# First-pair argmax by heads, bf16 one-hot in SBUF, four-pass similarities and a new order table

## The chip, the cores and the metric

The kernel runs on one core of a Trainium2 chip. The metric is device time in microseconds from the start to the end of one execution; for the kernel before it is 694.47 us, the median of three runs (694.42 to 694.76). In the text TensorE is PE, VectorE is DVE, ScalarE is ACT, GpSimd is POOL, and SP is the engine whose queue issues most DMAs.

## What is computed

Clustered attention over 2 batches x 8 heads, 768 tokens, 64 channels a head, and then two feed-forward blocks over the 1536 tokens. Only the attention is touched by the change:

```python
c_n = centroids / (norm(centroids) + 1e-06)            # 16 clusters for each head
q_assign = argmax(einsum('bhsd,hcd->bhsc', q_n, c_n))  # k_assign in the same way
mask = q_assign[:, :, :, None] == k_assign[:, :, None, :]
scores = where(mask, scale * q @ k.T, -1e9)
attn = softmax(scores); out = attn @ v
x = max(max(x @ w1, x @ w2), x @ w3) @ w_out           # first block
h = maximum(x @ w_in, 0); out = (h * h) @ w_out2       # second block
```

## The kernel before

**Numbers.** A value is held as two parts, hi (rounded to the fast matmul's format) and lo (the rest), so that a product takes three passes: hi by hi, hi by lo, lo by hi.

**Pairs.** Heads go in 8 pairs. For each pair q and k arrive (`load_qk`), are split into hi and lo (`p_rq`, `p_rk`, `p_lq`, `p_lk`), and are laid out per head by DMA into "stacks" (`p_stack`, tiles `ste` for the even head and `stodd` for the odd one). `p_sim` multiplies them with the centroids `cb`: six matmuls of 64x384 for each half of 384 tokens, accumulated in one PSUM bank (three for q, three for k). `p_simc` scales the result on ACT into SBUF (`simt`), `p_argt` transposes it on PE into PSUM, and five DVE instructions find the argmax: the maximum of each group of 16 (`p_arg0`), equal to it (`p_arg1`), times a descending weight (`p_arg2`), maximum again (`p_arg3`), equal to that (`p_arg4`). All of them work on the PSUM tile, and only the last writes a bf16 one-hot tile `oh`. `p_mkt` transposes the one-hot rows, and `p_mq`, `p_mk`, `p_m4`, `p_md` place them as 16 further rows of the stacks, where they add a large negative number to every pair of tokens in different clusters: the mask costs no pass of its own.

**The first pair** goes in two halves of 384 tokens (`hv`): its transposes, its five argmax steps and its mask rows run once for each half, and the halves alternate on DVE. The first score tile needs all of both.

**Score tiles.** Each head has 6 tiles of 128 queries, 96 in all. A tile `S` (`a_scores`) is four matmuls into a two-bank PSUM tile; there are two such tiles (ring "S", `psd`). DVE takes the row maximum (`a_max`, L738), ACT the exponential with its sum (`a_exp`, L745). Three tiles form a group: ACT and DVE make the reciprocals (`a_guard`, `a_rec`), POOL (at the start ACT) scales (`a_norm`), and for six blocks of 128 keys PE transposes (`a_tr`, L768), ACT and DVE split the block into hi and lo (`a_hi` L774, `a_lo` L779), and PE multiplies with v (`a_av`, L788 and L789). Transposes, similarities, argmax and mask transposes share three PSUM banks (ring "T", `pss`); a fourth bank collects the products with v.

**Warm-ups.** `warm(n)` (L325) issues n matmuls on the identity whose result is not used. `WARM` says how many stand at each place of the start.

**Order.** All steps of the attention are entries of a table `ops`; `ATT_ORDER` lists their numbers in the order in which they are issued. Each engine has one queue and works in that order. The feed-forward blocks follow, in an order that `arrange` works out; its first products (L425) already stand between the last attention steps.

Of the kernel before, what the change touches and what calls it, by code (L numbers as in the profile page):

```python
# [1439 lines left out]
```

## Time and profile before

| | before |
|---|---|
| median of three runs | 694.47 us |
| profiled execution, its own time | 693.93 us |
| its span, first to last instruction | 692.1 us |
| PE busy in the span | 676.9 us, 98% |
| DVE busy | 561.2 us, 81% |
| ACT busy | 501.1 us, 72% |
| POOL busy | 210.0 us, 30% |

The shares are averages over very different stages. The first 15 us bring in q and k of the first pair and find its clusters. From there to about 254 us the score tiles run; from 254 us on the feed-forward blocks do. A matmul's record reaches from its start to its result, so that records of neighbours overlap, and a busy PE is not a PE at its peak: the distance from start to start says what an instruction costs its queue. The same holds to a smaller degree for DVE and ACT.

### The profile page before, as it was taken

What the parts mean: (1) busy time and instruction counts of PE and PEld (TensorE: products, weight loads), DVE (VectorE), ACT (ScalarE), POOL (GpSimd) and SP (SyncE); (2) the same over time, 40 slices, a digit from 0 to 9 for tenths busy, and PEclk for the clock granted to TensorE, in tenths of its full rate; (3) what the DMA queues carried; (4) which work ended last, traced back from release to release, by engine and by line L of the source; (5) the groups of instructions that cost most, each with busy time, mean ns of one, the idle gap of its engine ahead of it and who ended that gap; (6) DMA issues with size and microseconds to landing.
All of it is one profiled execution on the core that took longest, in us unless ns stands there. A gap on an engine that the chain in (4) does not pass through costs nothing.

```text
span 692.1 us, 10148 instructions
## 1 busy us (share of the span) xinstructions
PE 676.9 (98%) x3531; PEld 577.3 (83%) x3531; DVE 561.2 (81%) x906; ACT 501.1 (72%) x977; POOL 210.0 (30%) x242
## 2 busy tenths in 40 slices
PE   7899999999999999999999999999999999999997
PEld 6689889899999878888888888888888888888885
DVE  6898999999999979998979659889679585968433
ACT  6899989899999865575545547798877786776610
POOL 6477987988769770100000000000000010000010
PEclk9999999999999999999999999999999999999999
DMA  7884553726432002211311231112211203120012
GB/s 207 198 234 119 120 161 91 189 58 147 111 89 91 1 1 93 91 62 61 103 66 61 76 121 62 61 62 82 101 62 61 98 27 115 48 79 1 1 73 111
DMA packets 22004, 62.21 MB, mean 90 GB/s; under 512 B 3616, under 2 KB 5280, under 8 KB 21504
## 3 DMA queue, kind: packets, MB, share of 16 engines
q1 hardware_dynamic: 21232, 59.98, 29.3%
q10 hardware_dynamic: 720, 1.57, 0.7%
q8 instruction: 28, 0.46, 0.3%
q14 instruction: 24, 0.20, 0.1%
HBM read 38.83 MB, written 3.15 MB: 61 GB/s over the span
## 4 chain that ended last, share of the span: by engine, by line
PE 62%; DVE 2%; issue 1%; ACT 1%; POOL 0%; ACTq 0%; POOLq 0%
PE pss L1066 23%; PE psn L1066 18%; PE pss L1321 10%; PE psn L1321 8%; PE pss L1142 1%; DVE acc_acc L1349 1%; DVE at L779 0%; DVE wtv L399 0%; PE pss L768 0%; ACT e L745 0%; PE pss L788 0%; PE pss L789 0%; POOL xT L822 0%; PE psn L1142 0%; PE psn L425 0%
## 5 line engine op out<-in xcount | busy, mean ns | idle before, releaser
L779 DVE TENSOR_TENSOR at<-pss,at 128x384 fp32r<-128x384 f32 x192 | 100.0, 548 | 13.1 <-ACT at L774 12.4
L763 POOL TENSOR_SCALAR e<-e,nm 128x768 f32<-128x768 f32 x93 | 85.6, 934 | 47.2 <-DVE nm L753 32.6
L738 DVE TENSOR_REDUCE nm<-psd 128x1 f32<-128x768 f32 x96 | 90.6, 948 | 5.4 <-PE psd L731 3.7
L774 ACT CAST at<-pss 128x384 fp32r<-128x384 f32 x192 | 86.5, 483 | 9.3 <-PE pss L768 7.4
L745 ACT ACTIVATE e<-psd,nm 128x768 f32<-128x768 f32 x96 | 87.3, 910 | 4.1 <-DVE nm L738 3.5
L768 PE MATMUL pss<-ident,e 128*128 128x128 f32 x576 | 86.5, 275 | 3.4 <-DVE at L779 1.7
L768 PEld LDWEIGHTS pss<-ident,e 128*128 128x128 f32 x576 | 68.6, 140 | 15.2 <-DVE at L779 5.0
L788 PE MATMUL pss<-at,vs 128*128 128x384 f32 x192 | 71.2, 371 | 0.5 <-ACT avt L801 0.5
L1321 PE MATMUL pss<-w_wh,g_g 128*128 128x512 f32 x216 | 71.4, 389 | 0.0
L789 PE MATMUL pss<-at,vs 128*128 128x384 f32 x192 | 65.8, 343 | 0.4 <-DVE at L779 0.3
L1057 POOL TENSOR_TENSOR t_tt<-a_a,t_tt 128x256 f32<-128x256 f32 x3 | 2.5, 848 | 191.5 <-DVE t_tt L1054 191.5
L1321 PE MATMUL psn<-w_wh,g_g 128*128 128x512 f32 (+1 forms) x172 | 56.5, 384 | 0.0
L1321 PEld LDWEIGHTS pss<-w_wh,g_g 128*128 128x128 f32 x216 | 40.5, 188 | 8.4
L1066 PE MATMUL pss<-xT,w_wh 128*128 128x512 f32 x140 | 43.1, 389 | 0.0
L1321 PE MATMUL pss<-w_wl,g_g 128*128 128x512 f32 x108 | 42.0, 389 | 0.0
L1042 ACT CAST w_wh<-a_a 128x1024 fp32r<-128x1024 f32 (+1 forms) x28 | 28.6, 1020 | 14.9 <-DVE a_a L1036 14.9
L789 PEld LDWEIGHTS pss<-at,vs 128*128 128x128 f32 x192 | 36.4, 189 | 3.0 <-DVE at L779 2.5
L1025 ACT ACTIVATE a_a<-raw_raw 128x512 f32<-128x512 f32 (+1 forms) x56 | 36.4, 653 | 3.3 <-DMA raw_raw<-w 1.3
L1321 PEld LDWEIGHTS psn<-w_wh,g_g 128*128 128x128 f32 x172 | 32.1, 188 | 6.4
L788 PEld LDWEIGHTS pss<-at,vs 128*128 128x128 f32 x192 | 36.2, 189 | 1.4 <-issue 0.5
L1027 ACT ACTIVATE r_r<-raw_raw 128x512 uint32<-128x512 uint32 (+1 forms) x56 | 36.5, 651 | 0.7 <-PE pss L1066 0.7
L1030 DVE SCALAR_TENSOR_TENSOR a_a<-raw_raw,a_a 128x512 uint32<-128x512 uint32 (+1 forms) x56 | 35.6, 668 | 0.5
(249 smaller groups left out, 1743.0 us busy)
## 6 DMA issues: line engine op xcount, KB each, us to landing
raw_raw<-w SPq DMA_DIRECT2D x16, 512.0 KB, 4.0
raw_raw<-win SPq DMA_DIRECT2D x16, 512.0 KB, 4.0
raw_raw<-wo SPq DMA_DIRECT2D x16, 512.0 KB, 3.6
raw_raw<-wo SPq DMA_DIRECT2D x8, 384.0 KB, 3.3
out<-acc_acc SPq DMA_DIRECT2D x11, 256.0 KB, 2.0
tv<-vv SPq DMA_DIRECT2D x7, 384.0 KB, 3.3
stodd<-rl SPq DMA_DIRECT2D x12, 192.0 KB, 5.5
stodd<-rl SPq DMA_DIRECT2D x4, 576.0 KB, 7.9
```

The costliest lines, as they stand in the source:

```text
L738: dve.tensor_reduce(nms[g][:, 0, i : i + 1], pss[s][:, :, :HS], axis=AX.XY, op=ALU.max, negate=True)
L745: act.activation(two(e), pss.pop(s)[:, :, :HS], AF.Exp, bias=nm[:, 0, i : i + 1], accum_out=nm[:, 1, i : i + 1])
L763: (pool if w == "P" else dve).tensor_scalar(e, e, r, 1.0, op0=ALU.mult, op1=ALU.mult)
L768: pe.transpose(pt[:, i * P : (i + 1) * P], et[3 * g + i][:, kt * P : (kt + 1) * P], ident)
L774: act.copy(a[:, 0, :], pts[g, kt][:, :HS])
L779: eng.tensor_tensor(a[:, 1, :], pts.pop((g, kt))[:, :HS], f(a[:, 0, :]), op=ALU.subtract)
L788: pe.matmul(avs[g][:, :HS], l, a[:, 0, :], start=kt == 0, stop=False)
L789: pe.matmul(avs[g][:, :HS], l, a[:, 1, :], start=False, stop=kt == NQ - 1)
L1025: op(("ab", u), due - 9, {A_: act_t(n) + 0.03}, lambda e, raw=raw, c=c: e.activation(T[a][:, c], f(T[raw][:, :n, 1]), AF.Abs), [("ld", u)] ...
L1027: op(("rd", u), due - 7.5, {A_: act_t(n) + 0.03}, lambda e, raw=raw, c=c: e.mul(u32(T[r][:, c]), T[raw][:, :n, 0], float(2.0**-29)), [("ld ...
L1066: pe.matmul(T[bank], T[w[wi]][:, wb * P : wb * P + P], x(xi), start=first and n == 0, stop=last and n == 3 * len(ks) - 1, skip_group_check ...
L1321: pe.matmul(T[bank][:, : n.stop - n.start], T["g", 2 * g + j, c][:, a_, i * P : i * P + P], T[wt, u][:, 512 * j + n.start : 512 * j + n.stop],
```

## The change

The first pair's argmax is taken by heads instead of by halves: the even head's five steps run over all 768 tokens (every second group of 16), then the odd head's. Its one-hot rows are transposed in four pieces, each into a PSUM tile of its own (k first half, k second half, q, and all for the odd head); q's piece goes to a two-bank score tile. The two mask rows of q and the two of k are divided anew between DVE and ACT. Score tile 1 goes to two banks of ring "T" instead of a two-bank tile (`SPLIT`), with two maxima, two exponentials and two small joining steps. For all pairs the equality, the weighting and the second maximum of the argmax now stand in the bf16 tile `oh` in SBUF. From pair 1 on (`WIDE`) a similarity half takes four matmuls instead of six: the hi and lo centroids stand side by side in `cb`, so that one pass over a hi input makes 128 rows (hi in one half of them, lo in the other), and a new DVE step `p_simd` adds the two halves of rows after ACT has scaled one of them. The first pair's first k remainder moves from DVE to POOL, two small steps of the centroid norm stand earlier, its scale is copied to four groups of 32 rows instead of two, and the warm-ups go from 98 to 70. Several `after` entries are dropped or changed, and the order table is new.

```diff
-WARM = 12, 34, 0, 28, 10, 14, 0
+WARM = 12, 24, 0, 34, 0, 0, 0
+SPLIT = 1,
-    "lk@0": "D", ...
+    "lk@0": "PD", ...
+WIDE = 1
 ATT_ORDER = [
-    4, 7, 5, 6, 11, 12, 8, 9, 50, 13, 20, 14, 0, 16, 22, 3, 21, 15, 23, 24, 25, 18, 33, 26, 2, 17, 34, 1, 27, 51, 19, 35,
+    4, 7, 6, 12, 5, 8, 11, 9, 13, 52, 20, 14, 0, 16, 22, 1, 21, 15, 23, 24, 18, 25, 2, 17, 26, 3, 27, 19, 53, 28, 29, 54,
...
-    cb = ac.tile([P, 2, HP, 96], F32R, name="cb")
+    cb = ac.tile([P, HP, 160], F32R, name="cb")
...
             ops = []
-            for w, hs, ls in ((slice(32, 96), 0, 3), (slice(0, 64), 1, 2)):
-                ops += [(cb[:, 0, hp, w], rl[:, hs, c]), (cb[:, 0, hp, w], rl[:, ls, c]), (cb[:, 1, hp, w], rl[:, hs, c])]
-            for i, (l, r) in enumerate(ops):
-                pe.matmul(pt[0:64, :HS], l, r, start=i == 0, stop=i == 5)
+            for w, hs, ls in ((32, 0, 3), (0, 1, 2)):
+                ops += [(w, 64, ls), (w, 128, hs)] if p >= WIDE else [(w, 64, hs), (w, 64, ls), (w + 64, 64, hs)]
+            ops.sort(key=lambda o: -o[1])
+            for i, (w, n, x) in enumerate(ops):
+                pe.matmul(pt[0:n, :HS], cb[:, hp, w : w + n], rl[:, x, c], start=i == 0, stop=i == len(ops) - 1, skip_group_check=True)
...
+        def p_simd(p, hf):
+            r = slice(64 * hf, 64 * hf + 64)
+            t = simt[p][r]
+            dve.scalar_tensor_tensor(t, psims[p, hf][r, :HS], scl[r, p % HP : p % HP + 1], t, op0=ALU.mult, op1=ALU.add)
...
-            dve.tensor_tensor(arg_in(p, c), arg_in(p, c), argm[p][:, c].unsqueeze(2).to_broadcast([P, n, NC]), op=ALU.is_equal)
+            dve.tensor_tensor(one_hot(p, o), arg_in(p, o), by_group(argm[p], o), op=ALU.is_equal)
...
-            dve.tensor_tensor(arg_in(p, c), arg_in(p, c), tieb.unsqueeze(1).to_broadcast([P, c.stop - c.start, NC]), op=ALU.mult)
+            t = one_hot(p, o)
+            dve.tensor_tensor(t, t, tieb.unsqueeze(1).to_broadcast([P, t.shape[1], NC]), op=ALU.mult)
...
+            if i == 2:
+                pt = pmk["q"] = rings["S"][1][:, 0, :].bitcast(BF16)
+            else:
+                pt = pmk["k", i] = ps_m(f"pmk{p}_{i}", BF16)
...
-            act.activation(st[0][64:80, 1, half(hf)], pmk[p][0:16, half(hf)], AF.Identity, bias=m4b[0:16], scale=m4s[0:16])
+            to, fr = st[0][64:80, 1, QS[i]], pmk["q"][0:16, QS[i]]
+            if i == 0:
+                dve.tensor_scalar(to, fr, BIG, -BIG, op0=ALU.mult, op1=ALU.add)
+            else:
+                act.activation(to, fr, AF.Identity, bias=m4b[0:16], scale=m4s[0:16])
...
-            dve.tensor_copy(st[0][64:80, 3, half(hf)], pmk["k"][0:16, half(hf)])
+            (act.copy if hf else dve.tensor_copy)(st[0][64:80, 3, half(hf)], pmk["k", hf][0:16, half(hf)])
...
+            if s in SPLIT:
+                pt = [ps_t(f"ps{s}_{hf}")[:, :HS] for hf in range(2)]
...
+            for hf, to in enumerate((m, part[:, 0:1])):
+                dve.tensor_reduce(to, pss[s][hf], axis=AX.X, op=ALU.max, negate=True)
+            dve.tensor_tensor(m, m, part[:, 0:1], op=ALU.min)
```

On DVE the first pair's argmax reads as follows before, from its first maximum (`mx`, `m` and `oh` are its maxima and its one-hot tile, `pss_69` the transposed similarities, `ste` the even head's stack, `nm` the score tiles' maxima):

```order
L653 TENSOR_REDUCE mx_247<-pss_69 128x12
L658 TENSOR_TENSOR pss_69<-pss_69,mx_247 128x192
L653 TENSOR_REDUCE mx_247<-pss_69 128x12
L662 TENSOR_TENSOR pss_69<-pss_69,tieb 128x192
L658 TENSOR_TENSOR pss_69<-pss_69,mx_247 128x192
L667 TENSOR_REDUCE m_295<-pss_69 128x12
L662 TENSOR_TENSOR pss_69<-pss_69,tieb 128x192
L673 TENSOR_TENSOR oh_299<-pss_69,m_295 128x192
L667 TENSOR_REDUCE m_295<-pss_69 128x12
L673 TENSOR_TENSOR oh_299<-pss_69,m_295 128x192
L697 CAST ste_228<-pss_71 16x384 x2
```

And now, on DVE from the same maximum to the first score tiles' maxima:

```order
L681 TENSOR_REDUCE mx_288<-pss_69 128x12
L684 TENSOR_TENSOR oh_294<-pss_69,mx_288 128x12x16
L688 TENSOR_TENSOR oh_294<-oh_294,tieb 128x12x16
L692 TENSOR_REDUCE m_299<-oh_294 128x12
L696 TENSOR_TENSOR oh_294<-oh_294,m_299 128x12x16
L681 TENSOR_REDUCE mx_288<-pss_69 128x12
L731 CAST ste_221<-pss_70 16x384
L726 TENSOR_SCALAR ste_221<-psd_80 16x128
L684 TENSOR_TENSOR oh_294<-pss_69,mx_288 128x12x16
L688 TENSOR_TENSOR oh_294<-oh_294,tieb 128x12x16
L692 TENSOR_REDUCE m_299<-oh_294 128x12
L779 TENSOR_REDUCE nm_340<-psd_76 128x1
```

The even head's one-hot rows are ready after five instructions instead of ten, and the odd head's five stand behind the first mask copies.

On ACT the same place before, from the copies that fill the even stack (`m` is the mask for the odd head, `e` the exponentials):

```order
L573 CAST ste_228<-rl_201 64x1536
L481 DMA tv_318<-vv 128x768
L694 ACTIVATE ste_228<-pss_70,m4b,m4s 16x384 x2
L702 ACTIVATE m_353<-pss_70,m4b,m4s 64x768
L745 ACTIVATE e_371,nm_360<-psd_76,nm_360 128x768
L745 ACTIVATE e_373,nm_360<-psd_80,nm_360 128x768
L619 ACTIVATE simt_379<-pss_69,scl 64x384
L745 ACTIVATE e_394,nm_360<-psd_76,nm_360 128x768
L749 ACTIVATE nm_360<-nm_360,guard 128x3
```

And now on ACT:

```order
L585 CAST ste_221<-rl_194 64x1536
L488 DMA tv_307<-vv 128x768
L728 ACTIVATE ste_221<-psd_80,m4b,m4s 16x640
L731 CAST ste_221<-pss_71 16x384
L792 ACTIVATE e_344,nm_340<-psd_76,nm_340 128x768
L736 ACTIVATE m_359<-pss_71,m4b,m4s 64x768
L795 ACTIVATE e_367,nm_340<-pss_69,nm_340 128x384
L795 ACTIVATE e_367,part<-pss_70,nm_340 128x384
L792 ACTIVATE e_374,nm_340<-psd_80,nm_340 128x768
L804 ACTIVATE nm_340<-nm_340,guard 128x3
```

One mask copy of k stands behind the long one of q, the odd head's mask stands behind the first exponential, and the second exponential is in two pieces.

## Rows read from the trace of the kernel before

**Rows 1.** Busy us of each engine by stretch (start:end, length; x instructions).

```profile
150.00:200.00 50.00, 49.92 (x334) 46.98 (x335) 46.99 (x85) 47.92 (x115) 39.68 (x43) 1.00 0.49 115
200.00:250.00 50.00, 48.50 (x304) 42.67 (x302) 46.53 (x80) 44.39 (x105) 39.03 (x40) 1.00 0.14 47
300.00:350.00 50.00, 50.00 (x222) 41.40 (x221) 47.14 (x68) 28.74 (x46) 0.74 (x1) 1.00 0.24 85
```

**Rows 2.** Timeline, two bursts on PE: start, length, engine, line, tiles, count.

```profile
124.86 1.08 PEld L768 LDWEIGHTS pss<-ident,e 128*128 128x128 f32 x9
...
127.07 1.22 PE L613 MATMUL pss<-xT,cb 128*64 128x384 f32 x6
```

**Rows 3.** PE's weight loads by line, 50 to 250: busy, mean | idle before.

```profile
L768 PEld LDWEIGHTS pss<-ident,e 128*128 128x128 f32 x516 | 61.8, 140 | 11.2 <-DVE at L779 4.1 <-POOL xr L810 0.9 <-POOL e L763 0.9
L789 PEld LDWEIGHTS pss<-at,vs 128*128 128x128 f32 x171 | 32.4, 189 | 2.8 <-DVE at L779 2.3
L788 PEld LDWEIGHTS pss<-at,vs 128*128 128x128 f32 x171 | 32.3, 189 | 1.4 <-issue 0.5 <-ACT avt L801 0.4
```

**Rows 4.** DVE by line, 50 to 250 us.

```profile
L779 DVE TENSOR_TENSOR at<-pss,at 128x384 fp32r<-128x384 f32 x172 | 89.5, 548 | 10.6 <-ACT at L774 10.0
L738 DVE TENSOR_REDUCE nm<-psd 128x1 f32<-128x768 f32 x81 | 76.6, 948 | 2.9 <-PE psd L731 2.2
```

**Rows 5.** DVE by line and shape, 0 to 260 us: the argmax and a remainder.

```profile
L658 DVE TENSOR_TENSOR pss<-pss,mx 128x384 f32<-128x384 f32 x7 | 3.9, 564 | 0.2
L662 DVE TENSOR_TENSOR pss<-pss,tieb 128x384 f32<-128x384 f32 x7 | 3.9, 559 | 0.0
L667 DVE TENSOR_REDUCE m<-pss 128x24 bf16<-128x384 f32 x7 | 3.9, 555 | 0.1
...
L559 DVE TENSOR_TENSOR rl<-tk,rl 128x384 fp32r<-128x384 f32 x2 | 1.1, 545 | 0.0
...
L662 DVE TENSOR_TENSOR pss<-pss,tieb 128x192 f32<-128x192 f32 x2 | 0.7, 366 | 0.1
```

**Rows 6.** Timeline from the first warm-ups to the second score tile.

```profile
1.68 1.46 PE L325 MATMUL pss<-identb 128*128 128x128 bf16 x12 [1.68 <-DVE identb L318]
...
3.73 3.23 PE L325 MATMUL pss<-identb 128*128 128x128 bf16 x34
...
6.77 2.29 PE L613 MATMUL pss<-rl,cb 128*64 128x384 f32 x12
...
8.19 0.58 ACT L619 ACTIVATE simt<-pss,scl 64x384 f32<-64x384 f32 x1 [1.13 <-DVE scl L503]
...
9.42 0.36 DVE L653 TENSOR_REDUCE mx<-pss 128x12 f32<-128x192 f32 x1 [1.33 <-PE pss L644]
...
9.93 0.37 PE L644 MATMUL pss<-ident,simt 64*128 64x64 f32 x3 [0.54 <-DVE mx L653]
...
10.23 1.74 PE L325 MATMUL pss<-identb 128*128 128x128 bf16 x28
...
13.13 0.34 PE L688 MATMUL pss<-identb,oh 128*32 128x128 bf16 x3 [1.16 <-DVE oh L673]
13.37 0.36 DVE L673 TENSOR_TENSOR oh<-pss,m 128x192 bf16<-128x192 f32 x1
...
15.02 1.22 ACT L694 ACTIVATE ste<-pss,m4b,m4s 16x384 fp32r<-16x384 bf16 x2 [2.61 <-PE pss L690]
...
16.82 0.52 PE L731 MATMUL psd<-ste 80*128 80x384 f32 x2
```

**Rows 7.** Timeline of ACT, the first exponentials and their scaling.

```profile
16.25 0.99 ACT L702 ACTIVATE m<-pss,m4b,m4s 64x768 fp32r<-64x768 bf16 x1
17.76 0.90 ACT L745 ACTIVATE e<-psd,nm 128x768 f32<-128x768 f32 x1 [0.52 <-DVE nm L738]
...
22.97 1.75 ACT L761 ACTIVATE e<-e,nm 128x768 f32<-128x768 f32 x2
...
28.41 0.92 ACT L745 ACTIVATE e<-psd,nm 128x768 f32<-128x768 f32 x1
```

More of the change, by code (lines that the diff above doesn't have):

```diff
@@ L290, in single_banks @@
     def single_banks(i):
-        pd[i].close()
-        one = ctx.enter_context(tc.tile_pool(name=f"pn{i}", bufs=1, space=PSUM, side=SIDES[i]))
+        o = (i + len(SPLIT)) % 2
+        pd[o].close()
+        one = ctx.enter_context(tc.tile_pool(name=f"pn{i}", bufs=1, space=PSUM, side=SIDES[o]))
         psu[i][:2] = [one.tile([P, 512], F32, name=f"psn{2 * i + j}") for j in range(2)]
@@ L498, in clustered_attention_moe @@
         cs = ap1.tile([P, 4], F32, name="cs")
-        scl = ap1.tile([64, HP], F32, name="scl")
+        scl = ap1.tile([P, HP], F32, name="scl")
         def c_scale(eng, i):
-            for r in (0, 32):
+            for r in range(0, P, 32):
                 eng.tensor_copy(scl[r : r + 32, i : i + 1], cs[32 * i : 32 * i + 32, 3:4])
@@ L516, in clustered_attention_moe @@
         ]
-        parts = [lambda o=o, r=r, c=c: act.copy(cb[r, 0, :, c], pcv[r, :, o, :]) for o, r, c in rc]
-        parts += [lambda o=o, r=r, c=c: dve.tensor_tensor(cb[r, 1, :, c], pcv[r, :, o, :], f(cb[r, 0, :, c]), op=ALU.subtract)
+        parts = [lambda o=o, r=r, c=c: act.copy(cb[r, :, c], pcv[r, :, o, :]) for o, r, c in rc]
+        parts += [lambda o=o, r=r, c=c: dve.tensor_tensor(cb[r, :, c.start + 64 : c.stop + 64], pcv[r, :, o, :], f(cb[r, :, c]), op=ALU.subtract)
                   for o, r, c in rc]
@@ L541, in p_rk @@
         def p_rk(p, hf=0):
+            prepared(p)
             c = halves(p)[hf]
@@ L669, in p_arg4, with of_head @@
-        def p_arg4(p, hf=None):
-            c = tiles_of(hf)[1]
-            o = once(oh, p, lambda: ap1.tile([P, NB_, NC], BF16, tag="oh", name=f"oh{p}"))
-            n = c.stop - c.start
-            dve.tensor_tensor(o[:, c], arg_in(p, c), argn[p][:, c].unsqueeze(2).to_broadcast([P, n, NC]), op=ALU.is_equal)
+        def of_head(t, o):
+            if o is None:
+                return t
+            return t.rearrange("p (u h) -> p u h" if len(t.shape) == 2 else "p (u h) c -> p u h c", h=2)[:, :, o]
@@ L675, in clustered_attention_moe, with p_mkt @@
         pmk, mrow = {}, {}
-        def p_mkt(p, hf=None):
-            pt = once(pmk, p, lambda: ps_m(f"pmk{p}", BF16))
+        def p_mkt(p, i=None):
             if p:
+                pt = pmk[p] = ps_m(f"pmk{p}", BF16)
                 o = oh[p].rearrange("p (t a) c -> p t (a c)", t=NQ // 2)
-                for i in range(NQ // 2):
-                    pe.transpose(pt[:, i * P : (i + 1) * P], o[:, i, :], identb)
+                for t in range(NQ // 2):
+                    pe.transpose(pt[:, t * P : (t + 1) * P], o[:, t, :], identb)
@@ new lines, in p_mkt, with p_mq @@
+            for t in range(NQ):
+                if i > 1 or t // (NQ // 2) == i:
+                    c = slice(0, 64) if i == 3 else slice(0, 16) if i == 2 else slice(32, 48)
+                    pe.transpose(pt[0 : c.stop - c.start, t * P : (t + 1) * P], o[:, t, c], identb)
+            if i == 3:
+                pmk[p] = pt
+            warm(WARM[4])
+        QS = [slice(0, P), slice(P, S)]
+        def p_mq(p, i):
+            to, fr = st[0][64:80, 1, QS[i]], pmk["q"][0:16, QS[i]]
[3 more added lines that the diff above has]
+                act.activation(to, fr, AF.Identity, bias=m4b[0:16], scale=m4s[0:16])
@@ L720, in clustered_attention_moe @@
         et, nms, pss, ats, avs, xraw, pts = {}, {}, {}, {}, {}, {}, {}
+        part = ap1.tile([P, 2], F32, name="part")
         def a_scores(s):
@@ L724, in a_scores @@
             t = st[h]
-            pt = ps_s(f"ps{s}")
+            if s in SPLIT:
+                pt = [ps_t(f"ps{s}_{hf}")[:, :HS] for hf in range(2)]
+            else:
+                pt = ps_s(f"ps{s}")
+                pt = [pt[:, hf, :HS] for hf in range(2)] + [pt[:, :, :HS]]
             k2 = slice(0, 80) if h % 2 == 0 else slice(0, 128)
@@ L744, in a_exp, with a_sum @@
             nm = nms[g]
-            act.activation(two(e), pss.pop(s)[:, :, :HS], AF.Exp, bias=nm[:, 0, i : i + 1], accum_out=nm[:, 1, i : i + 1])
+            pt, m, sm = pss.pop(s), nm[:, 0, i : i + 1], nm[:, 1, i : i + 1]
+            if s not in SPLIT:
+                act.activation(two(e), pt[2], AF.Exp, bias=m, accum_out=sm)
+                return
+            for hf, to in enumerate((sm, part[:, 1:2])):
+                act.activation(e[:, half(hf)], pt[hf], AF.Exp, bias=m, accum_out=to)
+        def a_sum(s):
+            g, i = divmod(s, 3)
+            sm = nms[g][:, 1, i : i + 1]
+            dve.tensor_tensor(sm, sm, part[:, 1:2], op=ALU.add)
         def a_guard(g):
@@ L870, in clustered_attention_moe @@
                      opens=[("sm", p, 0)] if hf == 0 else (), uses=[("T", "sim", p, hf), ("sm", p, 0)])
+                if p >= WIDE:
+                    pop_("simd", p_simd, (p, hf), [("simc", p, hf)], uses=[("T", "sim", p, hf), ("sm", p, 0)])
+            sims = [("simd" if p >= WIDE else "simc", p, h) for h in range(2)]
             for hf in hv:
-                first = hf != (1,)
-                sim = [("simc", p, h) for h in (hf or (0, 1))]
-                pop_("argt", p_argt, (p, *hf), sim, opens=[("T", "arg", p)] * first, uses=[("sm", p, 0), ("T", "arg", p)])
@@ new lines, in clustered_attention_moe @@
+            for o in [(0,), (1,)] if p == 0 else [()]:
+                first = o != (1,)
+                pop_("arg0", p_arg0, (p, *o), [("argt", p, *hf) for hf in hv], uses=[("T", "arg", p)])
+                pop_("arg1", p_arg1, (p, *o), [("arg0", p, *o)], opens=[("oh", p)] * first, uses=[("oh", p), ("T", "arg", p)])
+                pop_("arg2", p_arg2, (p, *o), [("arg1", p, *o)], uses=[("oh", p)])
+                pop_("arg3", p_arg3, (p, *o), [("arg2", p, *o)], uses=[("oh", p)])
+                pop_("arg4", p_arg4, (p, *o), [("arg3", p, *o)], uses=[("oh", p)])
@@ new lines, in clustered_attention_moe @@
+            if p == 0:
+                for i in range(4):
+                    pop_("mkt", p_mkt, (p, i), [("arg4", p, i // 3)] + [("mkt", p, i - 1)] * (i > 0), opens=[("T", "mk" if i == 3 else f"mk{i}", p)] * (i != 2), uses=[("oh", p)])
+                for hf in range(2):
+                    pop_("mk", p_mk, (p, hf), [("mkt", p, hf), ("stack", p, 0)], uses=[("T", f"mk{hf}", p)])
+                for i in range(2):
+                    pop_("mq", p_mq, (p, i), [("mkt", p, 2), ("stack", p, 0)])
+            else:
+                pop_("mkt", p_mkt, (p,), [("arg4", p)], opens=[("T", "mk", p)], uses=[("oh", p)])
```

117 lines of the change are left out of this document (55 added, 62 removed), and 143 rows, old and new, of tables (ATT_ORDER, ENG).

## The prediction

> **What bounds the kernel now.** I read the busy times by stretch first. From 300 us on, PE's records cover 50.00 of 50 us [rows 1]: a microsecond that the attention gives back before 254 us reaches the end, since the work behind it is PE's own and the change leaves its order alone. The question is what sets the pace before 254 us. There PE is again nearest to full, 49.92 of 50 us from 150 to 200, but ACT has 47.92 and DVE 46.99 in the same stretch [rows 1], so no engine has much room. PE's records overlap; two matmuls of 384 columns take 0.52 us and six take 1.22 [rows 2, 6], so one costs (1.22 - 0.52) / 4 = 0.175 us of the queue, and a transpose 1.08 / 9 = 0.12 us [rows 2]. From 50 to 250 us the weight loads of the transposes and of the two value products wait 11.2 + 2.8 + 1.4 = 15.4 us [rows 3]; part of that lies beside running matmuls. PE is thus full to something between 92 and 98%, and its largest named wait is for DVE's remainder (L779), which holds a bank of ring "T". DVE in turn stands idle 10.6 + 2.9 = 13.5 us there, 10.0 of it behind ACT's cast of the same bank [rows 4]. This is a loop of PE, ACT and DVE over three banks in which PE is tightest and DVE second. The start is another matter: there one chain decides, from the similarities through the argmax to the first score tile.
>
> **The first pair.** Before, the sims start at 6.77 us because 34 warm-ups stand ahead of them, the scale is ready for the first copy at 8.19, the second half's transposes end at 9.93 + 0.37 = 10.30, the last one-hot row at 13.37 + 0.36 = 13.73, and score tile 1 ends at 16.82 + 0.52 = 17.34 [rows 6]. Now ten warm-ups fewer free about 10 x 3.23 / 34 = 0.95 us of the queue, of which I take 0.55, as the remainders must be there too (POOL now makes one of them). The transposes then end at about 9.75. Five steps of 192 elements at 0.36 to 0.37 us [rows 5, 6] and a few hundredths between them make 2.0 us, so the even head's one-hot is there at 11.75, although it waits for both halves. Three transposes of one-hot rows took 0.34 us, the last one's way out in it [rows 6]; twelve at some 0.09 and that way out end at 13.0. Then ACT, in the order shown, makes 640 columns of q's mask (0.87 us, between 1.22 / 2 = 0.61 for 384 [rows 6] and 0.99 for 768 [rows 7]) and after it one half of k's (0.5): 14.4. The score tiles end at 14.6 and 15.2, 2.1 us earlier than before. The 34 warm-ups after the transposes (about 34 x 1.74 / 28 = 2.1 us [rows 6]) end at about 11.8, just as the one-hot is ready; where they run longer, they delay it by as much.
>
> Not all of the 2.1 us stays. Followed on, ACT makes the odd head's mask (0.99) between the first two exponentials, since DVE puts the last step of that argmax behind the first maximum; tile 1's exponential comes in two pieces; the group's guard waits for the sum's joining step, which is queued on DVE behind two maxima and a remainder. I get the group's scaling on ACT ending near 23.2 instead of 22.97 + 1.75 = 24.72, then both similarity copies of pair 1 (0.58 each, as at 8.19 [rows 6]) where one stood, and the seventh exponential at 27.75 by ACT's queue and 28.1 by DVE's, against 28.41 [rows 7]. DVE has by then done about 1 us more of pair 1's argmax. Between the 0.3 us at that mark and the 2.1 at tile 1, and with this 1 us, I take **-1.3 us**; bounds 0 and -2.5 (the 2.1 and the rest of the 0.95). The odd head's mask DMAs stand behind two loads of pair 2 on SP now; those rows are needed only at score tile 6, at about 25 us by this count, so I cost them at nothing; without that cover it is the time of the two loads.
>
> **Four-pass similarities.** Seven pairs, two halves, two matmuls fewer: 28 x 0.175 = 4.9 us off PE. It would all reach the end if PE were full alone. With PE at 92 to 98% and the other two engines close behind, I let 60% through: **-2.9 us**; bounds 0 and -4.9.
>
> **DVE.** `p_simd` adds 14 instructions on 64x384. The trace has none of its kind; the nearest are the remainders of the same length, 0.548 us [rows 4] and 0.545 from SBUF [rows 5]. Records of neighbours overlap by some 0.09 us, so 14 cost 6.4 to 7.7 us of DVE. Against it stands the argmax in bf16. From 384 to 192 elements the weighting falls from 559 to 366 ns [rows 5], about 1 ns an element; the remainder costs as much from SBUF (545) as the weighting from PSUM (559), so by rows the place alone buys nothing, and the gain is from 0 to what half the elements would save, 0.19 us for a step. I take that for the weighting alone: 7 x 0.19 = 1.3 us. DVE's net load is some 5 us more. It lies in the 13.5 us in which DVE stands idle [rows 4], so I cost it at **0**; bounds -1 and +5.2 (6.5 - 1.3), the latter if the idle time is tied to ACT's casts and can't be filled.
>
> The Trainium skill (VectorE: DVE Perf Modes, The perf-mode tier table) says that a two-tensor operation runs at twice the rate where all its tensors are 16-bit in SBUF, and that a reduction never does. By it the weighting is faster and the second maximum is not, which is what I took; the two equalities have an operand that is repeated or in fp32, and are left as they are. No run here shows a bf16 step in SBUF yet.
>
> **Banks.** A similarity bank is now held through ACT's copy and DVE's addition, about 0.6 us longer, 14 times: 8 us of bank time. The argmax bank is free after the second of five steps instead of the fifth, at least 3 x 0.56 us [rows 5] earlier, 7 times: 12 us. I cost the balance, and the new order behind the start, at 0, with 1 us to either side.
>
> **Sum.** -1.3 - 2.9 + 0 + 0 = -4.2 us. The profiled execution took 693.93 us, 1.83 more than its span and 0.54 less than the median of the runs; off the median, 694.47 - 4.2 = 690.3, and I say **690.2 us**. By the same steps its own range is 687.0 to 693.0.
>
> **The rivals.**
> 1. *DVE becomes the bound* (slower). If the 13.5 us of idle time are fixed by the hand-over from ACT (10.0 of them say so [rows 4]), DVE's added 5.2 us lengthen the attention, PE's saving turns into waits for banks, and only the start's 1.3 us is kept: 694.47 + 5.2 - 1.3 = 698.4. It decides from the point where DVE's idle time between 50 and 250 us would have to fall under about 9 us. For it: DVE is busy 46.5 to 47.0 of 50 us from 150 to 250 [rows 1]. Against it: that leaves 6 to 7%, and the wait at L779 is spread over short gaps, which a later step can fill.
> 2. *The PE saving is lost, the start's is not.* Waits for ring "T" take the place of the 28 matmuls: 694.47 - 1.3 = 693.2. For it: the load waits of 15.4 us [rows 3] show that banks, not only passes, set the pace.
> 3. *All of it counts.* -2.5 at the start and -4.9 on PE: 687.1. For it: PE's 49.92 of 50 us [rows 1], and freed argmax banks.
> 4. *The clock.* The granted clock of the stretches reads 1.00, which is 2.4 GHz [rows 1]; yet the first 12 warm-ups take 1.46 us and 28 later ones 1.74 [rows 6], so at the start one costs twice as much. If fewer warm-ups leave the first sims at that pace, 12 x 0.175 = 2.1 us come on top: 690.2 + 2.1 = 692.3. Against it: PE stays in work to the sims with 24 warm-ups too, and the stretch behind the argmax has more of them than before, not fewer.
>
> The Trainium skill (TensorE: Matmul & The Clock Gate, Why this matters for your kernels) speaks for rival 4: it asks for steady matmul work to reach the full clock and warns of idle gaps after it. In this trace PE stood idle for 1.16 us ahead of the one-hot transposes [rows 6] without a visible loss, so the trace does not bear the warning out at that length.
>
> **How the numbers follow.** Forecast 0.50, rival 1 0.14, rival 2 0.15, rival 3 0.18, rival 4 0.03. What a measurement can tell from no change is 0.2%, 1.4 us: 693.1 to 695.9. Faster is nearly all of the forecast, rival 3, a third of rival 2 and most of rival 4: 0.49 + 0.18 + 0.05 + 0.02 = 0.74. Same is the rest of these, 0.12; slower is rival 1, 0.14. The range reaches down to 686.2, below rival 3, and up to 695.2, which leaves out most of rival 1.
>
> **What the profile after would show.** The one-hot of the even head at about 11.8 us and score tile 1's end at about 15.2; the weighting at 0.37 us and the second maximum still at 0.55; 14 additions of about 0.55 us on DVE; four matmuls where a half of the similarities had six; the last attention product about 4 us earlier; and the feed-forward part as long as it was. I am wrong if DVE's idle time between 50 and 250 us shrinks by 5 us and PE's waits grow by as much (rival 1 or 2), or if the sims of the first pair start later than 6.77 us or take longer than 2.29 (rival 4).

## The result and the profile after

The changed kernel takes 699.86 us (median of 4 runs, 699.55 to 701.07) against 694.62 for the kernel before on the same chip (694.42 to 694.88); the ratio is 1.0082, interval 1.0069 to 1.0094. It is slower, by 5.2 us, and lies above the range that I gave. The forecast was wrong in its sign.

The profiled execution took 700.13 us, its span is 698.3, 6.2 longer than before. Where the span grew is read from the products with v, which both traces have 384 times in the same order (L788 and L789 before, L843 and L844 after), by the time at which the k-th of them starts: the 13th 41.70 before and 40.65 after, the 193rd 148.81 and 149.99, the 253rd 185.21 and 190.58, the last 253.58 and 259.39. So the changed kernel is 1.1 us ahead at 41 us, 1.2 behind at 149, 5.4 behind at 185 and 5.8 behind at the end of the attention. The part behind it, which the change leaves alone, added 0.4.

The stretches that answer to [rows 1] show the same place. Behind the length stand the busy times of PE, of PE's weight loads, of DVE, ACT and POOL, then the granted clock of TensorE, the share of the DMA engines and GB/s:

```profile
150.00:200.00 50.00, 46.57 (x296) 42.65 (x295) 47.74 (x79) 43.66 (x103) 35.47 (x39) 0.97 0.46 107
200.00:250.00 50.00, 49.04 (x315) 44.49 (x314) 45.73 (x82) 47.21 (x112) 40.25 (x43) 1.00 0.17 55
...
168.00:170.00 2.00, 0.15 (x1) 0.00 (x0) 2.00 (x1) 0.57 (x2) 2.00 (x4) 1.00 0.00 0
170.00:172.00 2.00, 0.67 (x5) 0.61 (x6) 2.00 (x3) 0.29 (x1) 2.00 (x2) 0.93 0.00 0
172.00:174.00 2.00, 2.00 (x10) 1.84 (x9) 1.22 (x3) 1.28 (x3) 0.13 (x1) 0.50 0.05 12
174.00:176.00 2.00, 2.00 (x12) 1.97 (x11) 1.66 (x4) 1.49 (x4) 0.62 (x1) 0.72 0.16 37
```

From 150 to 200 us PE works 46.57 us where it worked 49.92. In the rows of 2 us it is idle from 168 to 171.3, while DVE and POOL are both full, and then runs at a granted clock of 0.50, which is 1.2 GHz. The timeline around 167 us says what DVE did (start, length, engine, line, tiles, count, idle time ahead and what ended it):

```profile
166.25 1.00 POOL L863 TENSOR_TENSOR xr<-avt 64x384 f32<-64x384 f32 x1
167.24 2.66 POOL L818 TENSOR_SCALAR e<-e,nm 128x768 f32<-128x768 f32 x3
167.35 3.92 DVE L696 TENSOR_TENSOR oh<-oh,m 128x384 bf16<-128x384 bf16 x1
169.87 0.98 POOL L607 TENSOR_TENSOR vs<-tv,vs 128x384 fp32r<-128x384 f32 x1
170.82 1.31 POOL L863 TENSOR_TENSOR xr<-avt 64x384 f32<-64x384 f32 x1
171.33 0.34 PE L705 MATMUL pss<-identb,oh 128*128 128x128 bf16 x3 [3.18 <-DVE oh L696]
171.71 0.67 ACT L736 ACTIVATE m<-pss,m4b,m4s 128x384 fp32r<-128x384 bf16 x1 [3.14 <-PE pss L705]
```

One step, the last equality of pair 6's argmax, takes 3.92 us. It reads two operands in SBUF and starts 0.1 us into a run of five POOL instructions without a gap; it ends as the last of them is under way, and that one is the only long one (1.31 us where the same form took 1.00). PE has the transposes of that one-hot next in its queue and waits 3.18 us, ACT waits behind PE. The other steps of the kind, from 50 to 250 us (busy, mean ns), answer to [rows 4, 5]:

```profile
L834 DVE TENSOR_TENSOR at<-pss,at 128x384 fp32r<-128x384 f32 x165 | 85.6, 548 | 6.5 <-ACT at L829 5.8
L779 DVE TENSOR_REDUCE nm<-psd 128x1 f32<-128x768 f32 x81 | 76.7, 947 | 1.8 <-PE psd L770 1.5
L696 DVE TENSOR_TENSOR oh<-oh,m 128x384 bf16<-128x384 bf16 x6 | 8.1, 1356 | 0.0
L640 DVE SCALAR_TENSOR_TENSOR simt<-pss,scl,simt 64x384 f32<-64x384 f32 x10 | 6.1, 612 | 0.6 <-DMA ste<-m 0.2 <-ACT simt L635 0.2
...
L688 DVE TENSOR_TENSOR oh<-oh,tieb 128x384 bf16<-128x384 bf16 x6 | 4.3, 724 | 0.0
...
L692 DVE TENSOR_REDUCE m<-oh 128x24 bf16<-128x384 bf16 x6 | 3.2, 539 | 0.0
```

L688 (the weighting) and L696 (the last equality) have both operands in SBUF; their means, 724 and 1356 ns, are longer than that of the weighting in PSUM before (559 [rows 5]). Where POOL is idle they take 0.35 us (L688 at 132.65) and 0.55 (L696 at 115.72). L640 has one operand in PSUM and keeps to 612, L692 has one operand and keeps to 539. DVE's idle time behind the two largest groups is 6.5 + 1.8 us where it was 13.5 [rows 4].

The start, in the form of [rows 6, 7]:

```profile
6.19 3.05 PE L627 MATMUL pss<-rl,cb 128*64 128x384 f32 x12
7.51 1.73 PE L627 MATMUL pss<-rl,cb 128*64 128x384 f32 x8
...
9.90 0.40 PE L660 MATMUL pss<-ident,simt 64*128 64x64 f32 x3 [0.34 <-ACT simt L635]
...
11.12 0.26 DVE L688 TENSOR_TENSOR oh<-oh,tieb 128x192 bf16<-128x192 bf16 x1
...
11.75 0.83 POOL L548 TENSOR_SCALAR xT<-tq 128x768 fp32r<-128x768 f32 x1
11.80 0.98 DVE L696 TENSOR_TENSOR oh<-oh,m 128x192 bf16<-128x192 bf16 x1
...
13.72 0.88 ACT L728 ACTIVATE ste<-psd,m4b,m4s 16x640 fp32r<-16x640 bf16 x1 [1.13 <-PE psd L716]
...
14.63 0.28 DVE L726 TENSOR_SCALAR ste<-psd 16x128 fp32r<-16x128 bf16 x1 [0.79 <-ACT ste L728]
...
14.96 0.62 PE L770 MATMUL psd<-ste 80*128 80x384 f32 x2 [0.73 <-DVE ste L726]
...
15.81 0.52 PE L770 MATMUL pss<-ste 80*128 80x384 f32 x2
...
16.98 0.90 ACT L792 ACTIVATE e<-psd,nm 128x768 f32<-128x768 f32 x1 [2.03 <-DVE nm L779]
```

The even head's one-hot is ready at 12.78, where 11.75 was forecast. About half of the difference comes from the first similarities. They start 0.58 us earlier than before, but take 3.05 us instead of 2.29 [rows 6]: the second row is their last eight, in 1.73 us, so the first four took 1.32, 0.33 us each, about twice the 0.175 from start to start before. The transposes therefore end at 10.30, as before, and not at 9.75. The rest is the last step, which takes 0.98 beside POOL instead of 0.36. DVE's piece of q's mask then waits 0.79 us for ACT's piece. Score tile 1 ends at 16.33: 1.0 us earlier than before, where I had 2.1. And the clock falls, which it did not do before:

```profile
15.00:20.00 5.00, 4.06 (x20) 3.55 (x21) 4.63 (x10) 2.99 (x7) 1.87 (x3) 0.81 0.94 221
20.00:25.00 5.00, 4.24 (x19) 3.12 (x18) 3.34 (x7) 3.94 (x8) 2.28 (x3) 0.85 0.54 134
```

### The profile page after: what moved, and what is told of

It reads as the page before. It is cut to its first block, busy times and chain, and to the rows that moved or that the text cites. A ratio compares the mean times of both kernels' runs of the same rounds, so it can differ in the third digit from the quotient of the medians.

```text
span 698.3 us, 10072 instructions
## 1 busy us (share of the span) xinstructions
PE 676.8 (97%) x3481; PEld 575.8 (82%) x3481; DVE 571.4 (82%) x924; ACT 502.6 (72%) x979; POOL 212.2 (30%) x249
## 4 chain that ended last, share of the span: by engine, by line
PE 74%; DVE 16%; POOL 3%; ACT 3%; issue 2%; DMA 1%; SPq 1%; DVEq 0%; ACTq 0%; POOLq 0%
PE pss L1131 23%; PE psn L1131 18%; PE pss L1386 10%; PE psn L1386 8%; DVE nm L779 5%; DVE at L834 5%; PE pss L823 4%; PE pss L844 2%; PE pss L843 2%; PE psd L768 2%; PE psd L770 2%; POOL e L818 2%; DVE oh L696 1%; PE pss L627 1%; SPq L594 1%
## 5 line engine op out<-in xcount | busy, mean ns | idle before, releaser
L823 PE MATMUL pss<-ident,e 128*128 128x128 f32 x576 | 88.3, 278 | 5.2 <-DVE at L834 2.8
L843 PE MATMUL pss<-at,vs 128*128 128x384 f32 x192 | 71.1, 371 | 0.0
L844 PE MATMUL pss<-at,vs 128*128 128x384 f32 x192 | 65.8, 343 | 1.0 <-DVE at L834 1.0
L844 PEld LDWEIGHTS pss<-at,vs 128*128 128x128 f32 x192 | 36.5, 190 | 2.9 <-DVE at L834 2.5
L843 PEld LDWEIGHTS pss<-at,vs 128*128 128x128 f32 x192 | 36.3, 189 | 0.8
```

The lines of the kernel that those rows point to most:

```text
L823: pe.transpose(pt[:, i * P : (i + 1) * P], et[3 * g + i][:, kt * P : (kt + 1) * P], ident)
L843: pe.matmul(avs[g][:, :HS], l, a[:, 0, :], start=kt == 0, stop=False)
L844: pe.matmul(avs[g][:, :HS], l, a[:, 1, :], start=False, stop=kt == NQ - 1)
```

## The experiments

Theory P: a DVE step with two operands in SBUF waits for POOL's turn at a port that they share. The change turned 18 steps that read PSUM into such steps; they lengthen, and one meets POOL's longest run, starves PE and costs it the clock. Rival D: DVE is simply full (the 14 additions), and it does not matter where a step stands. Ratios are to the kernel before, timed beside each group of kernels, with their 95% intervals.

**The parts.** Four kernels; the kernel before took 694.47 us.

The last step of one pair right behind its second max:

```diff
+MOVED = [(("arg4", 5), ("arg3", 5))]
```


> One DVE step is moved: the last argmax step of pair 5 stands right behind its third step, 4.6 us earlier in DVE's queue, when POOL is idle. Theory P (a DVE step with two operands in SBUF waits while POOL works, and the 3.92 us of this one step made the gap on PE and the half clock behind it): the step takes 0.35 to 0.6 us, PE has no gap at 168 to 171 us, the granted clock stays 1.00 there, and the time is 694 to 696 us. Rival D (DVE is simply full, by the 14 additions): the gap shows up elsewhere and the time stays within 1 us of 699.9.

A miss of mine: the long step is pair 6's, so I moved the wrong one. 701.03 us, 1.0087 (1.0071 to 1.0103). The pair 6 step took 4.88 us here and the weighting of that pair 1.90.

The argmax of pairs 1 to 7 in PSUM again but for its last step's result (the order already gives the bank to another tile after the second step, so this kernel's masks are not the reference's):

```diff
+        def work(p, o):
+            return arg_in(p, o) if p else one_hot(p, o)
-            dve.tensor_tensor(one_hot(p, o), arg_in(p, o), by_group(argm[p], o), op=ALU.is_equal)
+            dve.tensor_tensor(work(p, o), arg_in(p, o), by_group(argm[p], o), op=ALU.is_equal)
...
```


> For pairs 1 to 7 the second, third and fourth argmax steps work in PSUM again, only the last writes the bf16 tile; the order stays that of the changed kernel. Theory P: none of these 14 steps is longer than 0.6 us any more, the 3.9 us wait is gone, 693 to 695.5 us, up to 1.5 us under the kernel with the one step moved. Rival D: 699 to 701. Rival B (banks of the ring set the pace, and the argmax now holds one for three steps longer): over 701.

698.36 us, 1.0053 (1.0037 to 1.0069), between the ranges of the two theories. The last step, which now reads PSUM, takes its normal time in the same run of POOL's. The next step with two SBUF operands behind it takes the wait:

```profile
168.78 0.55 DVE L698 TENSOR_TENSOR oh<-pss,m 128x384 bf16<-128x384 f32 x1
169.24 1.01 DVE L836 TENSOR_TENSOR at<-pss,at 128x384 fp32r<-128x384 f32 x2
170.17 2.40 DVE L565 SCALAR_TENSOR_TENSOR xT<-tq,xT 128x384 fp32r<-128x384 f32 x1
```

Six matmuls for pairs 1 to 7 again and no additions:

```diff
-                ops += [(w, 64, ls), (w, 128, hs)] if p >= WIDE else [...]
+                ops += [(w, 64, hs), (w, 64, ls), (w + 64, 64, hs)]
...
-            dve.scalar_tensor_tensor(t, psims[p, hf][r, :HS], scl[...], t, op0=ALU.mult, op1=ALU.add)
+            psims.pop((p, hf))
```


> Pairs 1 to 7 multiply with six matmuls again and the 14 additions on DVE are left out; all else, the order too, as in the changed kernel. Theory P: the long wait stays where POOL's burst still meets the step, 698 to 701 us. Rival D: 14 additions of 0.61 us are gone from the engine that sets the pace, 695 to 697 us, although PE has 28 matmuls more.

702.49 us, 1.0105 (1.0085 to 1.0126), above both ranges. Rival D asked for 695 to 697: with the 14 additions off DVE nothing is won here. But the step, now at 168.05, takes 4.86 us where it took 3.92, so this kernel does not weigh the additions by themselves.

The kernel before with the bf16 argmax in SBUF alone:

```diff
+            o = once(oh, p, lambda: ap1.tile([P, NB_, NC], BF16, tag="oh", name=f"oh{p}"))
-            dve.tensor_tensor(arg_in(p, c), arg_in(p, c), argm[p][:, c]..., op=ALU.is_equal)
+            dve.tensor_tensor(o[:, c] if p else arg_in(p, c), arg_in(p, c), argm[p][:, c]..., op=ALU.is_equal)
...
```


> The kernel before, in its own order, with only one part of the change: for pairs 1 to 7 the argmax from its second step on works in the bf16 tile in SBUF. Theory P: of the 14 two-operand steps several take 0.6 to 1.2 us instead of 0.56, since POOL is at work in most of these stretches, and the time rises by 0.5 to 3 us to 695 to 697.5; a burst of POOL steps next to one of them would give more. Rival D: these steps get shorter or stay, 693.5 to 694.8 us.

696.14 us, 1.0049 (1.0021 to 1.0077). In the old order too the move to SBUF costs time. How much is less sure: eight of the twelve runs took 695.21 to 696.62 us, four 701.73 to 703.27, and the trace is of one of the eight. The median is 1.7 us above the kernel before; the ratio, which weighs all twelve, says 0.2 to 0.8%. By line and form from 25 to 200 us, the two steps of two operands against the two that have at most one there:

```profile
L675 DVE TENSOR_TENSOR oh<-oh,m 128x384 bf16<-128x384 bf16 x7 | 5.4, 765 | 0.0
L664 DVE TENSOR_TENSOR oh<-oh,tieb 128x384 bf16<-128x384 bf16 x7 | 5.1, 727 | 0.0
...
L659 DVE TENSOR_TENSOR oh<-pss,mx 128x384 bf16<-128x384 f32 x7 | 3.9, 554 | 0.2
L669 DVE TENSOR_REDUCE m<-oh 128x24 bf16<-128x384 bf16 x7 | 3.8, 549 | 0.1
```

**The long step and the start.** The kernel before took 694.46 us.

```diff
+MOVED = [(("arg4", 6), ("arg3", 6))]
```


> The changed kernel with one instruction moved: the last argmax step of pair 6 (the one that took 3.92 us at 167.35) goes right behind the second max of its pair, where POOL stands idle for 2.7 us. Theory P (a step with two operands in SBUF waits for POOL's turn; that one wait made PE's gap of 3.2 us and the half clock behind it): the step takes 0.55 to 1.0 us, no PE gap over 2 us stands between 160 and 180, the clock of 150 to 200 is 0.99 or more, and the time is 694.5 to 697 (3 to 5 us less than the changed kernel). Rival D (DVE has no spare time in 50 to 250 whatever the place of a step, so the delay comes back elsewhere): 698.5 to 700. A step that still takes over 2.5 us would speak against my reading of when the port is free.

698.59 us, 1.0065 (1.0051 to 1.0078): 1.3 us less than the changed kernel where I expected 3 to 5, so 1.6 above P's range and inside D's. By the time alone D would have won. The trace says why little was gained: the step takes 0.56 us at 163.82, but the remainder step behind it falls into the same run of POOL's:

```profile
163.82 0.56 DVE L697 TENSOR_TENSOR oh<-oh,m 128x384 bf16<-128x384 bf16 x1
...
169.79 3.02 DVE L566 SCALAR_TENSOR_TENSOR xT<-tq,xT 128x384 fp32r<-128x384 f32 x1
```

The start (q's first mask piece ahead of the second, 14 warm-ups behind score tile 1):

```diff
+MOVED = [(("mq", 0, 1), ("mq", 0, 0))]
...
+            if s == 1:
+                warm(14)
```


> The changed kernel with its start mended alone: the first mask piece of the queries on DVE goes ahead of the second one on ACT (it waited 0.79 us for it), and 14 warm-up products stand behind the second score tile, in the gap of 0.94 us. The pair 6 step stays. Theory P with the start's own term (late mask 0.8 us, half clock from 17.5 to 22 some 1.5 us on PE): the first exp starts at 16.2 instead of 16.98, the clock of 15 to 25 is 0.95 or more, and the time is 697.5 to 699, 1 to 2 us less than the changed kernel. Rival (what the start gives is lost again before 100 us since DVE is full there, or the wait moves to another engine): 699.3 to 700.3.

699.23 us, 1.0073 (1.0055 to 1.0090), with a spread of 698.12 to 702.15, between the two ranges: inconclusive. The clock of 15 to 25 us was still 0.83 where I had asked for 0.95. Both edits:

> Both edits together: the pair 6 step behind its second max, and the mended start. Theory P: the two gains add up, 692.5 to 695.5, at or under the kernel before. Rival D (no spare time on DVE): 697.5 to 700.

697.14 us, 1.0042 (1.0030 to 1.0054), between the ranges of the two theories and nearer to D's. The remainder step took 3.97 us here.

The moved step with six matmuls:

> The moved pair 6 step with six matmuls in the similarities of pairs 1 to 7 again and without the 14 additions on DVE (everything else as in the changed kernel). It weighs the four passes with the long stall out of the way: against the kernel with the moved step alone it is slower by 1.5 to 3.5 us if the 4.9 us of matmuls that the four passes save count as I forecast (2.9), and it is within 0.5 us or faster if the 14 additions cost DVE as much as PE saves (rival 1 and rival D). By theory P 696.5 to 699.5.

697.78 us, 1.0046 (1.0034 to 1.0058): 0.8 less than its twin with four. The four passes gain nothing, which is the outcome set down for rivals 1 and D.

**Places and clock.** The kernel before took 694.70 us. In the first kernel the version with six matmuls has nine DVE instructions at places where POOL is idle in the trace:

```diff
+MOVED = [
+    (("arg4", 6), ("arg3", 6)), (("lq", 7, 0), ("arg4", 6)), (("arg2", 6), ("lo", 18, 1)), (("arg2", 2), ("arg1", 2)),
+    (("arg4", 2), ("lo", 4, 3)), (("lq", 4, 1), ("lo", 8, 0)), (("lq", 5, 1), ("arg4", 4)),
+    (("arg2", 7), ("arg1", 7)), (("arg4", 7), ("lo", 23, 1)),
+]
```


> The kernel with the moved pair 6 step and six matmuls (697.78), with eight more DVE instructions at other places and nothing else changed: the first remainder step of pair 7 (it took 3.97 us in place of the argmax step), the weightings of pairs 2, 6 and 7, the last steps of pairs 2 and 7, and the second remainder steps of pairs 4 and 5 stand where POOL is idle in that kernel's trace. Theory P (waits for POOL's turn cost the time; the work itself has room): no DVE step between 155 and 190 takes over 1.5 us, no PE gap over 1.2 us stands there, the end of attention is 3 to 5 us earlier, and the time is 693 to 695. Rival D (DVE is full, the place does not matter): 697 to 698.5. Rival W (the wait only moves on to the next step with two SBUF operands, as it did from the argmax step to the remainder step): a step of 3 us or more again, and 696.5 to 698.

696.16 us, 1.0013 (1.0002 to 1.0024), over P's range by 1.2 and below those of D and W. The three moved steps before the run of POOL's, and the stretch around it:

```profile
160.80 0.35 DVE L691 TENSOR_TENSOR oh<-oh,tieb 128x384 bf16<-128x384 bf16 x1
...
162.11 0.56 DVE L699 TENSOR_TENSOR oh<-oh,m 128x384 bf16<-128x384 bf16 x1
162.59 0.55 DVE L570 SCALAR_TENSOR_TENSOR xT<-tq,xT 128x384 fp32r<-128x384 f32 x1
```
```profile
150.00:200.00 50.00, 49.09 (x327) 45.48 (x327) 46.00 (x84) 47.05 (x113) 37.41 (x42) 1.00 0.45 108
```

None of them waits, no DVE step from 155 to 190 us takes over 1.5 us, and PE works 49.09 us of the stretch. With groups of warm-ups in the start's gaps on top:

```diff
+            warm(12 * (s == 0))
...
+            warm({1: 14, 5: 8}.get(s, 0))
...
+                warm(14 * (p == 1))
```


> The same with four groups of warm-up products in the start's gaps (12 inside the first score tile, 14 behind the second, 8 behind the sixth, 14 behind the similarity transposes of pair 1), which do not feed anything. If the half-clock stretches between 16 and 30 that came and went in the kernels so far (0.50 to 0.62 for about 4 us, at another place in each) come from these gaps, the granted clock of 15 to 50 is 1.00 in it and the time is 0.5 to 1.5 us under the kernel without the groups: 692 to 694. Rival (the half clock costs nothing since exp and DVE set the pace there): the same time within 0.4 us. If the groups are in the way: 0.5 to 1 us slower.

693.84 us, 0.9986 (0.9976 to 0.9995): the one version below the kernel before, by 0.14%. The mean granted clock is 0.998 or 0.999 in all 11 runs, where 10 of the 11 without the groups have 0.994 to 0.996. The eleventh of those has 0.999 and took 695.78 us, in the middle of 693.97 to 696.75; so that the groups pay through the clock is likely but not shown.

```profile
15.00:25.00 10.00, 9.51 (x76) 7.45 (x75) 7.77 (x17) 7.62 (x17) 5.01 (x7) 1.00 0.76 192
25.00:50.00 25.00, 24.31 (x164) 21.05 (x164) 22.86 (x42) 22.25 (x52) 16.03 (x19) 1.00 0.82 203
```

The same with four matmuls:

> The changed kernel (four matmuls and 14 additions) with the same eight moved places, the moved pair 6 step and the warm-up groups (the last of them behind the first transposes of the weights, where its own gap is). Theory P: 693 to 695.5, four to seven less than the changed kernel. Against its six-matmul twin: by theory A within 0.8 us of it or slower; by my forecast's term 2 to 3 us faster.

694.74 us, 1.0002 (0.9992 to 1.0012), 0.9 more than its six-matmul twin. The four passes alone in the kernel before I tried with the additions too late: they read banks that another tile had taken, so its 706.54 us say nothing.

```diff
+                ops += [(w, 64, ls), (w, 128, hs)] if p else [(w, 64, hs), (w, 64, ls), (w + 64, 64, hs)]
...
+                while n < 2 and todo[at][:2] != ("argt", p):
+                    n += todo[at][0] in ("mx", "lo", "lq", "rec")
+                    at += 1
+                todo.insert(at, ("simd", p, hf))
```


> The kernel before with one part of the change alone: four matmuls in the similarities of pairs 1 to 7, the 14 additions on DVE two instructions behind their ACT copy, the argmax as it was. My forecast's term says 2.9 us less (691.6, bounds 689.6 to 694.5). Theory A (the 14 additions of 0.6 us cost DVE as much as PE saves, as the pair of kernels with the moved step hinted, 698.59 with four against 697.78 with six): 694 to 695.3.

**Passes alone and warm-ups alone.** The kernel before took 694.58 us. First the four passes in the kernel before, with each addition ahead of the next use of its bank:

```diff
+                own = todo.index(("sim", p, hf))
+                taken = sum(x[0] in ("T", "sim", "argt", "mkt") for x in todo[own + 1 : at])
...
+                    if taken == 3 or todo[at][:2] == ("argt", p):
+                        break
```


> The kernel before with the four matmuls and the 14 additions alone, each addition up to two DVE instructions behind its ACT copy but ahead of the next use of its bank (in the try before this one it stood behind that, and the numbers said nothing). My forecast's term: 691.6 (2.9 less, bounds 689.6 to 694.5). Theory A (the additions on DVE and the longer hold of the bank cost what the 28 matmuls save): 693.9 to 695.5.

706.67 us, 1.0168 (1.0154 to 1.0182): 12 us slower, which neither theory had. The old order has no room for the additions; from 25 to 200 us PE waits for them and for the remainders behind them (total us, times, longest; L775 and L648 are transposes, L614 the similarities):

```profile
PE pss L775 <- DVE simt L626: 6.4, 7, 1.4
PE pss L775 <- DVE at L786: 2.7, 6, 0.7
PE pss L614 <- DVE simt L626: 2.1, 2, 1.4
PE pss L648 <- DVE simt L626: 1.7, 1, 1.7
```

Then the groups of warm-ups alone:

> The changed kernel with the four groups of warm-up products in the start's gaps and every DVE step where the change has it. If the half clock of the start costs 1 to 2.5 us (2.3 by the pair of kernels with six matmuls, 696.16 and 693.84): 697.3 to 699, clock 1.00 from 15 to 50, and the step of 3 to 5 us near 167 stands as it was. If the groups only paid together with the moved places: 699.5 to 700.5.

701.90 us, 1.0095 (1.0079 to 1.0111): a miss. The clock of 15 to 50 us is 1.00, but the step near 169 takes 3.93 us and the weighting ahead of it 1.90 instead of 0.92; in this profiled execution the loss from the 193rd to the 253rd product is 5.2 us where it was 4.2.

**Places alone, and POOL's work moved.** The kernel before took 694.08 us. First the places alone with four matmuls, then the change's own order with POOL's work taken away instead of the step.

> The changed kernel with the eight moved places and the moved pair 6 step, without the warm-up groups; four matmuls and 14 additions as in the change. Theory P with the start's clock as a term of its own: 696 to 698, that is 2 to 4 less than the changed kernel for the places alone, and 1 to 3 more than with the groups (694.74). If the groups do nothing by themselves (as the kernel with the groups alone says, 701.90 against 699.86): 694 to 695.5.

696.34 us, 1.0038 (1.0024 to 1.0051), as expected. Its warm-up twin is 1.6 us faster.

```diff
-    "nrm@31": "PAP"
+    "nrm@31": "PAP", "nrm@20": "AAA"
```


> The changed kernel with every DVE step at its own place, but the three scalings of the twentieth group (they start at 167.24 on POOL, beside the 3.92-us step) on ACT, which stands idle from 168.6 to 171.7. POOL's row is then 2.66 us shorter. Theory P: the step takes 1.4 to 2.7 us instead of 3.92, PE's gap is under 2 us, and the time is 697 to 699.2. A rival by which the step is long for a reason of DVE's own (its operands, a semaphore, its form) leaves it at 3.5 us or more, and the time at 699.5 to 701.

698.54 us, 1.0061 (1.0049 to 1.0074), inside P's range; a cause of DVE's own would have left 699.5 or more. The step stands where the change put it and takes 1.29 us, PE has no gap over 1 us from 150 to 190, and the clock of 150 to 200 us is 1.00:

```profile
168.19 1.01 POOL L607 TENSOR_TENSOR vs<-tv,vs 128x384 fp32r<-128x384 f32 x1
168.33 1.29 DVE L696 TENSOR_TENSOR oh<-oh,m 128x384 bf16<-128x384 bf16 x1
169.16 1.33 POOL L863 TENSOR_TENSOR xr<-avt 64x384 f32<-64x384 f32 x1
```

## Why the prediction was wrong

**The step that failed** is the one on DVE: "by rows the place alone buys nothing", with the result costed at 0. I compared a step from SBUF (545 ns) with one from PSUM (559) [rows 5] and asked only what SBUF gains. That row comes from the first microseconds and was not delayed by POOL; the kernel before has the same kind of step beside POOL, and there it shows the price:

```profile
53.49 1.25 DVE L553 SCALAR_TENSOR_TENSOR xT<-tq,xT 128x384 fp32r<-128x384 f32 x1
58.71 0.54 DVE L553 SCALAR_TENSOR_TENSOR xT<-tq,xT 128x384 fp32r<-128x384 f32 x1
```

The first of the two stands beside three scalings on POOL, the second beside none. In the attention POOL works 39 to 40 of 50 us [rows 1], so of 14 steps moved to SBUF most had to meet it. The Trainium skill says as much (SBUF — State Buffer, SBUF: two separate sides): DVE and GpSimd take one port pair as a lock, and a DVE step with two SBUF inputs stands still while a GpSimd instruction that reads SBUF holds it. The traces agree (0.35 us alone, 0.92 beside POOL for the weighting of pair 6), and go further: a step can lose the turn to four instructions in a row.

What the wait cost is shown from both sides. Nine DVE steps at other places bring the changed kernel from 699.86 to 696.34 (1.0082 to 1.0038), and the same order with 2.66 us of POOL's work elsewhere brings it to 698.54 with a step of 1.29 us for 3.92. The bf16 argmax alone costs the kernel before 1.7 us by the medians; in its trace 1.6 us are lost from the 13th to the 193rd product with v, the stretch in which the changed kernel lost 2.2. Of these 2.2 the moved places give back 0.4 in their trace, so most of the loss ahead of the long step stays open. That the half clock behind PE's gap of 3.2 us is part of the price is read from the trace; no run held it apart from the gap.

**The four passes**: -2.9 us forecast; nothing gained. Six matmuls instead of four are 0.8, 0.9 and 0.2 us faster in three pairs of kernels: 698.59 and 697.78, which is within the noise; 694.74 and 693.84, whose warm-up groups differ in one place; 696.34 and 696.16, as ratios 1.0038 and 1.0013. The changed kernel and its twin with six matmuls go the other way (699.86 and 702.49), but the long step is 3.92 us in one and 4.86 in the other. PE did save its matmuls. Where the saving went is read from the third pair, by the weight loads of the transposes from 50 to 250 us, four matmuls first:

```profile
L828 PEld LDWEIGHTS pss<-ident,e 128*128 128x128 f32 x506 | 59.8, 140 | 13.7 <-DVE at L839 6.9 <-DVE simt L645 0.7 <-POOL xT L874 0.6
L826 PEld LDWEIGHTS pss<-ident,e 128*128 128x128 f32 x508 | 61.1, 140 | 10.3 <-DVE at L837 4.7 <-POOL e L821 0.6 <-issue 0.2
```

They wait 3.4 us longer, 2.2 of it for DVE's remainder, which frees a bank of ring "T"; DVE's idle time behind its two largest groups is 10.5 us instead of 15.7. So DVE had room for the additions, as I had said, but freed the banks later. I had costed the banks at 0; this is the mechanism of rival 2, to which I gave 0.15. In the old order the additions alone cost 12 us.

**The start**: -1.3 us forecast. Score tile 1 came 1.0 us earlier, not 2.1. Nearly all of the difference stands ahead of the even head's one-hot: the slow first similarities (0.55 us) and the port wait of 0.62 us in the last step. DVE's piece of q's mask waits 0.79 us for ACT's. The 13th product is still 1.1 us ahead.

**Rival 4**, to which I gave 0.03, was right in kind. Its mark was that the first similarities take longer than 2.29 us, and they took 3.05, 0.8 us more; I had priced 2.1 for all twelve. It is no accident of one trace: in all 14 traces of kernels with 24 warm-ups ahead of them, one to ten of the twelve matmuls run at the slow pace (2.47 to 3.79 us for the twelve); in the four traces with 34 none does (2.28 to 2.29). My argument against it, that PE stays in work with 24 warm-ups too, did not hold. The column of the granted clock reads 1.00 there, as it does for the first warm-ups; only the times of the matmuls show it. A second stretch, which I had not looked for, came at 18 to 22 us, where that column shows half clock (0.53 and 0.62) and two score tiles and the similarities of pair 1 run in it. I had read from one gap of 1.16 us in the kernel before that such gaps cost nothing; behind it stood 24 warm-ups among the mask's pieces, which the change removed. Groups of warm-ups behind it are worth 1.6 and 2.3 us (696.34 to 694.74, 696.16 to 693.84) once the long waits are gone. With those in place the same groups gave no gain (701.90), and why the weighting of pair 6 waits longer there I can only argue: the start moves DVE against POOL.

With the places and the warm-ups together the changed kernel (694.74) is level with the one before. So even there nothing is left of the 4.2 us that the start and the passes were to bring.

**Rival 1** had the time closest (698.4), and its mark was passed: DVE's idle time fell to 8.3 us. But its mechanism is not the one found for the loss. With the same additions on DVE and nine steps at other places the time fell to 696.34, and DVE's full load had room. That the passes' saving turned into waits is the part of it that holds.

**Right** were the shorter weighting where POOL is idle (0.33 to 0.35 us, 0.37 forecast), the second max that stays at 0.54, the additions near 0.6, and the feed-forward part.
